# Seven products instead of eight for the second channel product too, in batches 3 to 7 of a fused attention, mixer and gated-MLP kernel

## The chip, the cores and the metric

The kernel runs on one core of one Trainium2 chip. The time is device microseconds of one launch. The engines are named as in the profile: PE (TensorE, matrix products), PEld (its weight loads), DVE (VectorE), ACT (ScalarE), POOL (GpSimd), SP (SyncE, which issues the transfers). PSUM is the memory that PE writes products into; SBUF is the on-chip memory for everything else.

## The reference

Eight batches of 576 tokens and 512 channels go through three blocks in float32, each batch by itself:

```
out  = softmax(q k^T / 8) v          # 8 heads of 64, in chunks of 64 tokens; then x[S=576, 512]
u    = x + (relu(x^T w_tok1) w_tok2)^T           # w_tok1 576x256, w_tok2 256x576
y    = u + relu(u w_ch1) w_ch2                   # w_ch1 512x1536, w_ch2 1536x512
a, v = split(relu(y w_in), 2)                    # w_in 512x1024
g    = a * (w_spatial @ layernorm(v) + b_spatial)
out  = g w_out                                   # 512x512
```

The two products with w_ch1 and w_ch2 are called ch1 and ch2 below. `h` is relu(u w_ch1), 1536 rows by 576 tokens in the transposed form in which the kernel holds it.

## The kernel before

Each float32 operand is held as two f16 numbers, a high part and the rest (hi and lo), and each product of two matrices is made as three PE products: hi·hi, hi·lo, lo·hi. Channels lie on the 128 partitions, tokens along the row, in two halves of 288. One matmul is 128 weights by 128 rows by 288 columns (the first three products) or 512 columns (the others).

One batch passes these stages in the order in which PE is to run them: ch1, ch2, blocks of the output product of the batch before (`proj`, L779, 12 matmuls of 512 columns, called a proj block here), the two halves of the gated MLP's first product (`gate_v` L702 and `gate_u`), then the token mixing of the next batch (tok1 L466, tok2), the spatial product with its multiplication (`gated`, L754 and L766), and then ch1 of the next batch. The attention of a later batch (steps such as L225, L241, L242, L251 to L254, L295 and L296) is cut into about 100 steps, which are placed between the matmuls by a counter of PE columns; the table PACE (L499) says how quickly that counter runs in each stage.

PE's order is the order in which the code issues. The order on DVE, ACT and POOL is made by a scheduler from priorities (`tc.high_priority`) and the times it expects, and each of these engines then works strictly in that order.

From batch 2 on, ch1 (`ch1_fast`, L615) treats the row tiles in six pairs. The weights of a pair form a 2x2 matrix of blocks, and so do the channels and tokens of u; the four block products of h that a 2x2 product needs, eight in the usual way, come from seven products of sums of blocks, called A11, A12, A22, S1, S2, S3, S4 here (the code before has them by numbers 0 to 6). A product of a pair is six matmuls. Four intermediate results are added by DVE: u2 (L645), v (L660), the block c22 (L661) and the two blocks c (L652). ACT applies relu in place (L634), copies the high parts (L503), POOL subtracts for the low parts (L504). The sums of the weights are made once, in batch 1, laid down in DRAM (`c1s`), and streamed by SP through 18 slots of 512 columns (L578). The sums of u are made behind tok2 (`first_sums`, L509 to L523).

The order of one pair p on PE is A11(p), S2(p), S4(p-1), A22(p-1), S1(p), S3(p), A12(p). The two results of a PSUM tile d are S1 and S3 of p; S4(p) is added onto S1's half, so it may begin only when v and c22 have read d. This is the line on which S4 waits:

```
DVE.tensor_tensor(out=vb, in0=d[:, 0, 0:288], in1=u2b[p % 2], op=ALU.add)      # L660
DVE.tensor_tensor(out=c22, in0=d[:, 1, 0:288], in1=vb, op=ALU.add)             # L661
```

ch2 (L669) is the usual product in every batch: 288 matmuls of 288 columns with weights that stay in SBUF (L676), and a residual addition (L535 to L537) for each of the four row tiles.

PSUM tiles come from one ring of four two-bank tiles (`mp`), which attention's scores and outputs use too.

Of the kernel before, what the change touches and what calls it, by code (L numbers as in the profile page):

```python
# [26 lines left out]
def mixer_kernel(ctx: ExitStack, tc, qk0, qk, v, wt1, wt2, wc1, wc2, win, wsp, bsp, wout, out):  # L27
# [471 lines left out]
    PACE = {"first": 0.5, "pair": 0.8, "ch1": 1.0, "ch2": 1.2, "gate": 1.0, "tok1": 1.0, "last": 0.6}  # L499
# [82 lines left out]
    used = [0]

    def sum_steps(p):
        f = vals[:, 0:1024].rearrange("p (k m) -> p k m", k=4)
        s = vals[:, 1024:2048].rearrange("p (n k m) -> p n k m", n=4, k=2)
        g = vall[:, 0:2048].rearrange("p (n e k m) -> p n e k m", n=4, e=2, k=2)
        a11, a12, a21, a22 = f[:, 0:2, 0:128], f[:, 2:4, 0:128], f[:, 0:2, 128:256], f[:, 2:4, 128:256]
        w = c1w[:, :, p]
        o = c1s[p].rearrange("p (n e k m) -> p n e k m", n=7, e=2, k=2)  # L590
# [24 lines left out]
    def ch1_fast():  # L615
        t1, t2 = slice(0, 288), slice(288, 576)
# [3 lines left out]
        def product(o, p, n, b, start):  # L620
            assert ORDER[used[0] % 42] == (p, n)
            i = used[0] % SLOTS * 512
            w = call[:, i:i + 512].rearrange("p (e k m) -> p e k m", e=2, k=2)
            o = o[:, 0:288]
            for k in range(2):
                for i, (a, e) in enumerate(((0, 0), (0, 1), (1, 0))):
                    PE.matmul(out=o, lhsT=w[:, a, k], rhs=b[:, e, k], start=(start and k + i == 0),  # L627
                              stop=(k == 1 and i == 2), skip_group_check=not start)
                    pump(288)
            used[0] += 1  # L630
            stream(used[0] + SLOTS)

        def relu2(c, hi, lo):
            ACT.activation(out=c, in_=c, func=AF.Relu)  # L634
            split(c, hi, lo, POOL)

        for p in range(7):
# [8 lines left out]
            if p:
                d, u = cd[p - 1], u2b[(p - 1) % 2]
                product(d[:, 0], p - 1, 6, xb[:, :, 2:4, t2], False)
                product(d[:, 1], p - 1, 2, tq[3], False)
                c = wrk.tile([128, 2, 288], F32, tag="t", name="c")  # L650
                with high():
                    DVE.tensor_tensor(out=c, in0=d[:, :, 0:288], in1=u.rearrange("p (a t) -> p a t", a=1).to_broadcast([128, 2, 288]), op=ALU.add)  # L652
                    relu2(c, hb[:, p - 1, 0, 1:3], hb[:, p - 1, 1, 1:3])
            if p < 6:
                cd[p] = d = pm.tile([128, 2, 512], F32, tag="m", name="mp")
                c22 = c22b[p % 2]
                product(d[:, 0], p, 3, tq[0], True)
                product(d[:, 1], p, 5, tq[2], True)
                with high():
                    DVE.tensor_tensor(out=vb, in0=d[:, 0, 0:288], in1=u2b[p % 2], op=ALU.add)  # L660
                    DVE.tensor_tensor(out=c22, in0=d[:, 1, 0:288], in1=vb, op=ALU.add)  # L661
                    relu2(c22, hb[:, p, 0, 3], hb[:, p, 1, 3])
                product(a[:, 0], p, 1, xb[:, :, 2:4, t1], False)
                with high():
                    x1, hi, lo = a[:, 0, 0:288], hb[:, p, 0, 0], hb[:, p, 1, 0]
                    ACT.activation(out=hi, in_=x1, func=AF.Relu)
                    DVE.scalar_tensor_tensor(out=lo, in0=x1, scalar=0.0, in1=hi, op0=ALU.max, op1=ALU.subtract)
# [310 lines left out]
```

## Time and profile before

| | |
|---|---|
| three runs | 1149.47, 1152.74, 1153.25 us; median 1152.74 |
| profiled execution | 1149.73 us, span 1147.9 us |
| granted TensorE clock | 0.995 of full speed over the span |
| PE, DVE, ACT, POOL busy | 96%, 57%, 40%, 30% of the span |

The span runs from the first to the last instruction of the profiled execution. PE is busy nearly all the time, so time is lost or won where PE works or where it waits; the other engines matter by what they make PE wait for. Matmuls follow one another faster than a single one lasts, so the cost of a matmul is read from a long run of them, not from the mean duration of one.

### The profile page before, as it was taken

Reading aid. Unit: us, or ns where it says so; the run is one execution under the profiler, and the core shown is the slowest. Engines: PE = TensorE matmul, PEld = TensorE weight load, DVE = VectorE, ACT = ScalarE, POOL = GpSimd, SP = SyncE. Lnnn points to the kernel's source line nnn. Section 1 sums busy time; section 2 is a strip of 40 time slices with the busy share of each in tenths; the row PEclk is TensorE's granted clock in tenths of the full one; section 3 lists DMA queues with packets and bytes.
Section 4 is the critical chain, followed back from the end, with each engine's and each line's share of the span. In section 5 each row is a group of like instructions: output and inputs, shape, how many; then the busy total and the mean of one; then the engine's idle time right before and its main releaser. Section 6 shows DMA issues by size and latency. Waiting matters only on the chain.

```text
span 1147.9 us, 26048 instructions
## 1 busy us (share of the span) xinstructions
PE 1106.4 (96%) x11040; PEld 787.2 (69%) x11040; DVE 651.1 (57%) x1117; ACT 458.6 (40%) x798; POOL 344.6 (30%) x328
## 2 busy tenths in 40 slices
PE   6898999999999999999999999999999999999998
PEld 5576757776577756777567765677657775677765
DVE  7999987666485245744466534763258422562132
ACT  3334444444346233553345423463244612343131
POOL 0000033334254212642235322453135421252021
PEclk9899999999999999999999999999999999999999
DMA  9487521565037250463314532255222612030001
GB/s 320 143 251 238 194 62 29 134 153 157 15 75 188 59 128 3 108 163 72 96 29 129 141 81 70 38 153 129 79 43 71 171 32 61 5 98 14 19 19 46
DMA packets 139108, 115.27 MB, mean 100 GB/s; under 512 B 81520, under 2 KB 122992, under 8 KB 136688
## 3 DMA queue, kind: packets, MB, share of 16 engines
q1 hardware_dynamic: 138992, 113.62, 36.8%
q8 instruction: 86, 1.41, 0.5%
q14 instruction: 30, 0.25, 0.1%
HBM read 84.48 MB, written 14.94 MB: 87 GB/s over the span
## 4 chain that ended last, share of the span: by engine, by line
PE 74%; DVE 18%; issue 3%; ACT 2%; DMA 2%; POOL 1%; SPq 0%; DVEq 0%; ACTq 0%; POOLq 0%
PE mp L676 22%; PE mp L450 16%; PE mp L627 14%; PE mp L779 8%; PE mp L702 7%; PE mp L473 4%; DVE gb L147 2%; DVE gb L143 2%; DVE gt L754 1%; PE mp L234 1%; DVE xT L509 1%; PE mp L280 1%; DVE gb L141 1%; DVE gt L766 1%; DVE qk L225 1%
## 5 line engine op out<-in xcount | busy, mean ns | idle before, releaser
L676 PE MATMUL mp<-hb,c2w 128*128 128x288 f16 x2304 | 289.6, 286 | 4.5 <-DVE c2w L156 4.4
L676 PEld LDWEIGHTS <-c2w 128*128 128x128 f16 x2304 | 222.6, 98 | 62.2 <-DVE c2w L156 5.7
L627 PEld LDWEIGHTS <-c1w 128*128 128x128 f16 x1512 | 147.2, 98 | 50.3 <-issue 13.3
L627 PE MATMUL mp<-xb,c1w 128*128 128x288 f16 x864 | 125.1, 286 | 11.2 <-DVE vn L645 9.0
L450 PE MATMUL mp<-spw,vn 128*128 128x288 f16 x896 | 112.3, 286 | 0.0
L450 PEld LDWEIGHTS <-vn 128*128 128x128 f16 x896 | 87.1, 98 | 22.0
L450 PE MATMUL mp<-xb,inw 128*128 128x288 f16 x768 | 99.4, 286 | 0.6 <-ACT vt L712 0.4
L537 POOL TENSOR_TENSOR xb<-rt,xb 128x576 f16<-128x576 f32 x22 | 29.9, 1359 | 223.6 <-ACT xb L536 223.6
L779 PE MATMUL mp<-otw,gb 128*128 128x512 f16 x432 | 95.4, 379 | 0.0
L450 PEld LDWEIGHTS <-inw 128*128 128x128 f16 x768 | 74.8, 98 | 24.7 <-issue 1.0
L702 PE MATMUL mp<-inw,xb 128*128 128x512 f16 x384 | 88.2, 379 | 0.5 <-ACT xb L536 0.3
L450 PE MATMUL mp<-xb,c1w 128*128 128x288 f16 x576 | 73.8, 286 | 4.4 <-DVE xb L530 2.5
L535 DVE SCALAR_TENSOR_TENSOR rt<-mp,xT 128x576 f32<-128x576 f32 x32 | 24.1, 754 | 93.5 <-PE mp L676 93.5
L779 PEld LDWEIGHTS <-gb 128*128 128x128 f16 x432 | 42.0, 98 | 48.8
L504 POOL TENSOR_TENSOR hb<-c,hb 128x576 f16<-128x576 f32 x36 | 46.1, 1281 | 95.4 <-ACT hb L503 95.4
L718 DVE BATCH_NORM_STATS2 st<-vt 128x6 f32<-128x512 f32 (+1 forms) x40 | 27.5, 690 | 81.2 <-ACT vt L712 76.8
L450 PEld LDWEIGHTS <-c1w 128*128 128x128 f16 x576 | 55.3, 98 | 19.9 <-DVE c1w L156 3.0
L536 ACT ACTIVATE xb<-rt 128x576 f16<-128x576 f32 x32 | 21.9, 684 | 117.0 <-DVE rt L535 117.0
L262 POOL TENSOR_TENSOR p<-sd,p 128x512 f16<-128x512 f32 (+1 forms) x30 | 36.8, 1226 | 97.2 <-ACT p L259 85.8
L702 PEld LDWEIGHTS <-xb 128*128 128x128 f16 x384 | 37.2, 98 | 41.8 <-DVE xb L537 0.7
L627 PE MATMUL mp<-c1w 128*128 128x288 f16 x432 | 64.7, 286 | 0.0
L769 POOL TENSOR_TENSOR gb<-gt,gb 128x576 f16<-128x576 f32 x31 | 48.4, 1566 | 47.0 <-ACT gb L768 47.0
(183 smaller groups left out, 1656.6 us busy)
## 6 DMA issues: line engine op xcount, KB each, us to landing
c1w<-c1s SPq DMA_DIRECT2D x252, 128.0 KB, 2.3
qk<-in_qk SPq DMA_DIRECT2D x96, 128.0 KB, 2.9
out<-o SPq DMA_DIRECT2D x31, 256.0 KB, 2.0
v<-in_v SPq DMA_DIRECT2D x56, 128.0 KB, 2.9
vn<-in_wc SPq DMA_DIRECT2D x4, 1024.0 KB, 5.2
otw<-in_wc SPq DMA_DIRECT2D x3, 1024.0 KB, 4.9
spw<-in_wc SPq DMA_DIRECT2D x3, 1024.0 KB, 5.5
c1s<-vn SPq DMA_DIRECT2D x6, 512.0 KB, 2.9
```

What stands on the lines that cost most here:

```text
L262: POOL.tensor_tensor(out=p_hl[rows, 1], in0=m["sd"][rows], in1=p_hl[rows, 0], op=ALU.subtract)
L450: PE.matmul(out=o, lhsT=l, rhs=r, start=(i == 0), stop=(i == len(seq) - 1))
L473: PE.matmul(out=pss[m], lhsT=l, rhs=r, start=(i + j == 0), stop=False)
L504: eng.tensor_tensor(out=lo, in0=t, in1=hi, op=ALU.subtract)
L535: keep("d", DVE.scalar_tensor_tensor(out=t, in0=ps, scalar=DN10, in1=two(x[:, m]), op0=ALU.mult, op1=ALU.add))
L537: eng.tensor_tensor(out=xl, in0=t, in1=xh, op=ALU.subtract)
L627: PE.matmul(out=o, lhsT=w[:, a, k], rhs=b[:, e, k], start=(start and k + i == 0), stop=(k == 1 and i == 2), skip_group_check=not start)
L676: PE.matmul(out=o, lhsT=c2w[:, a, k, mc], rhs=hb[:, k // 2, r, k % 2 * 2 + t], start=(k + e == 0), stop=(k == 11 and e == 2))
L702: PE.matmul(out=ps, lhsT=l, rhs=r, start=(k + e == 0), stop=(k == 3 and e == len(seq) - 1))
L718: keep("d", DVE.bn_stats(out=st[0:n], in_=t[0:n]))
L769: eng.tensor_tensor(out=gl, in0=t, in1=gh, op=ALU.subtract)
L779: PE.matmul(out=ps, lhsT=gb[:, l, k, tk], rhs=otw[:, r, k], start=(k == 0 and e == 0), stop=(k == 3 and e == 2))
```

## The change

In batches 3 to 7 ch2 is made by seven products per 2x2 block as well. There h takes the part that u has in ch1: besides its four blocks, seven sums and blocks in all are needed in hi and lo for each pair of row tiles, and they are made pair by pair inside `ch1_fast`: xs holds the four blocks in float32, t13 is one DVE subtraction of 576 columns, t24 two of 288, and POOL makes the low parts of the pieces. The results go to the memory that h and the resident ch2 weights had (`hF`). ch2 then is 14 products of 18 matmuls. The sums of w_ch2 are made in batch 2 and laid down in DRAM (`c2s`), and 42 pieces per batch are streamed through the same 18 slots as those of ch1. From batch 2 on, two proj blocks move from behind ch2 to behind the third and the sixth pair of `ch1_fast`; in batches of five blocks the fifth moves to just before `gated`. The order of the gate tiles changes, and PACE has other numbers.

```diff
+    A11, A12, A22, S1, S2, S3, S4 = range(7)
+    ORDER2 = [(0, A11), (1, A11), (0, A12), (1, A12), (0, S2), (0, S1), (0, S3), (1, S2), (1, S1), (1, S3), (0, S4), (0, A22), (1, S4), (1, A22)]
+    FIRST_FAST, FIRST_FULL = 2, 3
+    hF = [t[:, 4032 * i:4032 * (i + 1)].rearrange("p (n e t) -> p n e t", n=7, e=2) for t in (hall, c2all) for i in range(3)]
+    c2s = tc.dram_tile([2, 7, 128, 1536], F16, name="c2s")
...
-    PACE = {"first": 0.5, "pair": 0.8, "ch1": 1.0, "ch2": 1.2, "gate": 1.0, "tok1": 1.0, "last": 0.6}
+    PACE = {"first": 0.2, "pair": 0.8, "ch1": 1.0, "ch2": 1.3, "gate": 1.0, "tok1": 1.0, "last": 0.3}
...
+        pieces += [(1, p, n, 0) for p, n in ORDER1]
+        if b >= FIRST_FULL:
+            pieces += [(2, q, n, k) for q, n in ORDER2 for k in range(3)]
...
+                    c = xp[:, 1:4:2] if full else new_work("c")
+                    DVE.tensor_tensor(out=c, in0=d[:, :, 0:288], in1=spread(u), op=ALU.add)
+                    if full:
+                        f = hF[p - 1]
+                        ACT.activation(out=c, in_=c, func=AF.Relu)
+                        split(xp[:, 2:4], f[:, 1:3, 0], f[:, 1:3, 1], POOL)
+                        t13, t24 = new_work("t13"), new_work("t24")
+                        DVE.tensor_tensor(out=t13, in0=xp[:, 1:3], in1=xp[:, 0:2], op=ALU.subtract)
+                        DVE.tensor_tensor(out=t24[:, 0], in0=xp[:, 2], in1=t13[:, 0], op=ALU.subtract)
+                        DVE.tensor_tensor(out=t24[:, 1], in0=xp[:, 3], in1=t24[:, 0], op=ALU.subtract)
+                        split(t13, f[:, 3:5, 0], f[:, 3:5, 1], POOL)
+                        split(t24, f[:, 5:7, 0], f[:, 5:7, 1], POOL)
...
+                    if full:
+                        xp = xs[p % 2][:, 0]
+                        ACT.activation(out=xp, in_=x1, func=AF.Relu)
+                        split(xp, hF[p][:, 0, 0], hF[p][:, 0, 1], DVE)
...
+            if p in between:
+                between[p]()
+
+    def ch2_fast(x):
+        def product(o, n, start):
+            q, m = next(order)
+            for j in range(3):
+                w = weights_of(2, q, n, j)
+                fast_product(o, w, lambda e, k: hF[2 * j + k][:, blocks[n], e], start and j == 0, j == 2, start)
...
             if b >= FIRST_FAST:
-                ch1_fast()
+                early = pend[:2]
+                pend = pend[2:]
+                ch1_fast(b >= FIRST_FULL, {5 - 3 * k: (lambda i=i: proj(b - 1, i)) for k, i in enumerate(early)})
...
+            if b == FIRST_FULL - 1:
+                sum_pump([(2, p, vall) for p in range(4)], 2000.0)
+            if b >= FIRST_FULL:
+                ch2_fast(x)
...
-            for i in pend:
+            for i in pend[:2]:
                 proj(b - 1, i)
+            if b == FIRST_FULL - 1:
+                sum_end()
+                sum_pump([(2, p, hall) for p in range(4, 6)], 4500.0)
```

On PE the change is plain from this: ch2 of five batches has 252 matmuls instead of 288, and proj blocks stand between pairs. On the other engines the scheduler decides. In batch 7, where no attention is left, DVE's rows from one pair's c to the next stood like this before (L660 and L661 are v and c22, L667 the low part of the block from A12, L645 is u2):

```order
L652 TENSOR_TENSOR c_13386<-mp_13326,vn_97 128x576 [waits PE_49,Pool_49]
L660 TENSOR_TENSOR vn_97<-mp_13391,vn_97 128x288 [waits DVE_49,PE_49]
L661 TENSOR_TENSOR vn_97<-mp_13391,vn_97 128x288 [waits DVE_49]
L667 SCALAR_TENSOR_TENSOR hb_95<-mp_13355,hb_95 128x288 [waits Activation_49]
L645 TENSOR_TENSOR vn_97<-mp_13420,vn_97 128x288 [waits Activation_49]
L652 TENSOR_TENSOR c_13451<-mp_13391,vn_97 128x576 [waits PE_49,Pool_49]
```

and now like this (L713 is c, L719 t13, L732 v, L720 and L721 the two parts of t24, L733 c22, L510 the low part, L706 u2):

```order
L713 TENSOR_TENSOR vn_97<-mp_13766,vn_97 128x2x288 [waits PE_49]
L719 TENSOR_TENSOR t13_13829<-vn_97 128x576 [waits Activation_49,Pool_49]
L732 TENSOR_TENSOR vn_97<-mp_13838,vn_97 128x288 [waits DVE_49,PE_49]
L720 TENSOR_TENSOR t24_13830<-vn_97,t13_13829 128x288 [waits DVE_49,Pool_49]
L733 TENSOR_TENSOR xs_100<-mp_13838,vn_97 128x288 [waits DVE_49]
L721 TENSOR_TENSOR t24_13830<-vn_97,t24_13830 128x288 [waits DVE_49]
L510 TENSOR_TENSOR hb_95<-xs_100,hb_95 128x288 [waits Activation_49]
L706 TENSOR_TENSOR vn_97<-mp_13882,vn_97 128x288 [waits Activation_49]
L713 TENSOR_TENSOR xs_100<-mp_13838,vn_97 128x2x288 [waits PE_49]
```

Three instructions of the pair before, t13 and the parts of t24, have come between c and c22 and between c22 and the next u2, and t13 waits for ACT.

ACT's rows of the same stretch were (L644 copies A11's result for u2, L634 is relu, L503 the high part):

```order
L644 ACTIVATE vn_97<-mp_13420 128x288 [waits PE_49]
L634 ACTIVATE c_13451<-c_13451 128x576 [waits DVE_49]
L503 ACTIVATE hb_95<-c_13451 128x576 [waits Activation_49]
L666 ACTIVATE hb_95<-mp_13420 128x288 [waits PE_49]
L634 ACTIVATE vn_97<-vn_97 128x288 [waits DVE_49]
L503 ACTIVATE hb_95<-vn_97 128x288 [waits Activation_49]
L644 ACTIVATE vn_97<-mp_13485 128x288 [waits PE_49]
```

and are now (L716 relu of c, the three L509 after it high parts, L743 and L735 relus, L948 the copy of a proj block, L705 the copy for u2):

```order
L716 ACTIVATE vn_97<-vn_97 128x2x288 [waits DVE_49]
L509 ACTIVATE hb_95<-vn_97 128x2x288 [waits Activation_49]
L509 ACTIVATE hb_95<-t13_13829 128x2x288 [waits DVE_49]
L743 ACTIVATE xs_100<-mp_13794 128x288 [waits PE_49]
L509 ACTIVATE hb_95<-xs_100 128x288 [waits Activation_49]
L735 ACTIVATE xs_100<-xs_100 128x288 [waits DVE_49,Pool_49]
L509 ACTIVATE hb_95<-t24_13830 128x2x288 [waits DVE_49]
L948 ACTIVATE o_13879<-mp_13866 128x512 [waits DMAHW1_49,PE_49]
L705 ACTIVATE vn_97<-mp_13882 128x288 [waits PE_49]
```

The copy for the next u2 stands behind the copy of t24, which waits for DVE.

At the start of ch1 of batch 3, DVE's last rows ahead of the first u2 were (L252 to L254 are attention, L754 and L766 the spatial product's multiplication):

```order
L252 TENSOR_SCALAR mx_6453<-mx_6453 128x8 [waits DVE_49]
L766 TENSOR_TENSOR gt_6054<-gt_6054,hb_95 128x576 [waits DVE_49]
L253 RECIPROCAL mx_6453<-mx_6453 128x8 [waits DVE_49]
L254 TENSOR_TENSOR sd_6201<-sd_6201,mx_6453 128x512 [waits DVE_49]
L754 SCALAR_TENSOR_TENSOR gt_6095<-mp_6061,bB_83 128x576 [waits PE_49,Pool_49]
L766 TENSOR_TENSOR gt_6095<-gt_6095,hb_95 128x576 [waits DVE_49]
L754 SCALAR_TENSOR_TENSOR gt_6133<-mp_6102,bB_83 128x576 [waits PE_49,Pool_49]
L766 TENSOR_TENSOR gt_6133<-gt_6133,hb_95 128x576 [waits DVE_49]
L645 TENSOR_TENSOR vn_97<-mp_6140,vn_97 128x288 [waits Activation_49]
```

and are now (L258 to L261 attention, L913 and L925 the multiplication):

```order
L258 TENSOR_REDUCE mx_6665<-sd_6418 128x8 [waits Activation_49]
L259 TENSOR_SCALAR mx_6665<-mx_6665 128x8 [waits DVE_49]
L260 RECIPROCAL mx_6665<-mx_6665 128x8 [waits DVE_49]
L261 TENSOR_TENSOR sd_6418<-sd_6418,mx_6665 128x512 [waits DVE_49]
L913 SCALAR_TENSOR_TENSOR gt_6226<-mp_6197,bB_83 128x576 [waits PE_49,Pool_49]
L925 TENSOR_TENSOR gt_6226<-gt_6226,hb_95 128x576 [waits DVE_49]
L706 TENSOR_TENSOR vn_97<-mp_6233,vn_97 128x288 [waits Activation_49]
```

Between the attention's last step and u2 one multiplication stands where there were two.

In the last pair of batch 4, DVE's rows from one c to the next were

```order
L652 TENSOR_TENSOR c_8445<-mp_8376,vn_97 128x576 [waits PE_49]
L660 TENSOR_TENSOR vn_97<-mp_8450,vn_97 128x288 [waits DVE_49,PE_49]
L661 TENSOR_TENSOR vn_97<-mp_8450,vn_97 128x288 [waits DVE_49,Pool_49]
L667 SCALAR_TENSOR_TENSOR hb_95<-mp_8409,hb_95 128x288 [waits Activation_49]
L652 TENSOR_TENSOR c_8495<-mp_8450,vn_97 128x576 [waits PE_49]
```

and from c22 to the next c and t13 are now

```order
L733 TENSOR_TENSOR vn_97<-mp_8613,vn_97 128x288 [waits DVE_49]
L249 TENSOR_TENSOR sd_8782<-mp_8620,mx_8781 128x2x4x64
L232 TENSOR_TENSOR qk16_86<-qk32_85,qk16_86 128x8x64 [waits DMAHW4_49,DMAHW3_49,DMAHW7_49,DMAHW2_49,Activation_49]
L510 TENSOR_TENSOR c2w_79<-vn_97,c2w_79 128x288 [waits Activation_49]
L258 TENSOR_REDUCE mx_8941<-sd_8782 128x8 [waits Activation_49]
L259 TENSOR_SCALAR mx_8941<-mx_8941 128x8 [waits DVE_49]
L260 RECIPROCAL mx_8941<-mx_8941 128x8 [waits DVE_49]
L261 TENSOR_TENSOR sd_8782<-sd_8782,mx_8941 128x512 [waits DVE_49]
L713 TENSOR_TENSOR vn_97<-mp_8613,vn_97 128x2x288 [waits PE_49]
L719 TENSOR_TENSOR t13_8735<-vn_97 128x576 [waits Activation_49,Pool_49]
```

Six attention steps, which before stood one pair earlier, now stand between the last c22 and the last c.

## Rows read from the trace of the kernel before

**Rows 1.** The page, part 1: busy time, share of the span, instructions

```profile
PE 1106.4 (96%) x11040; PEld 787.2 (69%) x11040; DVE 651.1 (57%) x1117; ACT 458.6 (40%) x798; POOL 344.6 (30%) x328
```

**Rows 2.** Waits of PE: line, what it waited for, total, times, longest

```profile
PE mp L627 <- DVE vn L645: 9.0, 5, 2.1
...
PE mp L627 <- DVE vn L661: 2.3, 6, 0.4
```

**Rows 3.** Chain of waits of batch 7: start, length, what

```profile
1047.13 35.28 PE mp L676 x288
1082.41 7.77 PE mp L779 x36
```

**Rows 4.** Timeline, one pair of batch 4 without attention: start, length, engine, line

```profile
623.74 0.46 DVE L661 TENSOR_TENSOR vn<-mp,vn 128x288 f32<-128x288 f32 x1
...
625.19 0.90 PE L627 MATMUL mp<-xb,c1w 128*128 128x288 f16 x6
625.39 0.41 ACT L644 ACTIVATE vn<-mp 128x288 f32<-128x288 f32 x1 [0.23 <-PE mp L627]
...
625.83 0.46 DVE L645 TENSOR_TENSOR vn<-mp,vn 128x288 f32<-128x288 f32 x1 [1.01 <-ACT vn L644]
...
626.86 0.76 DVE L652 TENSOR_TENSOR c<-mp,vn 128x576 f32<-128x576 f32 x1 [0.57 <-PE mp L627]
```

**Rows 5.** Timeline, last pair of batch 4

```profile
640.40 0.46 DVE L661 TENSOR_TENSOR vn<-mp,vn 128x288 f32<-128x288 f32 x1
...
640.92 0.90 PE L627 MATMUL mp<-xb,c1w 128*128 128x288 f16 x6 [0.38 <-DVE vn L661]
```

**Rows 6.** Groups of DVE by shape: busy, mean ns, idle before

```profile
L225 DVE TENSOR_TENSOR qk<-qk,qk 128x1024 f16<-128x1024 f32 x24 | 32.7, 1363 | 0.6 <-ACT qk L222 0.6
L766 DVE TENSOR_TENSOR gt<-gt,hb 128x576 f32<-128x576 f32 x32 | 30.0, 937 | 1.0
L652 DVE TENSOR_TENSOR c<-mp,vn 128x576 f32<-128x576 f32 x36 | 27.2, 755 | 19.5 <-PE mp L627 19.5
...
L754 DVE SCALAR_TENSOR_TENSOR gt<-mp,bB 128x576 f32<-128x576 f32 x32 | 24.0, 751 | 14.8 <-PE mp L450 12.6 <-POOL gb L772 1.5
...
L254 DVE TENSOR_TENSOR sd<-sd,mx 128x512 f32<-128x512 f32 x24 | 16.8, 698 | 0.5
...
L242 DVE TENSOR_TENSOR sd<-mp,mx 128x512 f32<-128x512 f32 x24 | 16.5, 686 | 0.5
...
L251 DVE TENSOR_REDUCE mx<-sd 128x8 f32<-128x512 f32 x24 | 16.3, 678 | 3.5 <-ACT sd L246 3.5
```

**Rows 7.** Groups of POOL by shape

```profile
L504 POOL TENSOR_TENSOR hb<-c,hb 128x576 f16<-128x576 f32 x36 | 46.1, 1281 | 95.4 <-ACT hb L503 95.4
...
L504 POOL TENSOR_TENSOR hb<-vn,hb 128x288 f16<-128x288 f32 x36 | 26.4, 734 | 1.9 <-ACT hb L503 1.9
```

**Rows 8.** Groups of ACT by shape

```profile
L634 ACT ACTIVATE c<-c 128x576 f32<-128x576 f32 x36 | 24.7, 685 | 55.6 <-DVE c L652 55.2
L503 ACT ACTIVATE hb<-c 128x576 f16<-128x576 f32 x36 | 24.6, 683 | 1.0
...
L644 ACT ACTIVATE vn<-mp 128x288 f32<-128x288 f32 x36 | 14.7, 408 | 7.3 <-PE mp L627 7.3
```

**Rows 9.** Timeline of POOL, sums of u before ch1 of batch 2

```profile
321.88 1.60 POOL L299 TENSOR_TENSOR xh<-xT,xh 128x512 f16<-128x512 f32 x1 [1.30 <-issue]
324.89 3.44 POOL L504 TENSOR_TENSOR c1w<-q,c1w 128x576 f16<-128x576 f32 x2 [1.41 <-ACT c1w L503]
```

**Rows 10.** Timeline of DVE, the same stretch

```profile
322.39 1.71 DVE L519 TENSOR_TENSOR q<-xT,q 128x576 f32<-128x576 f32 x1
324.02 0.75 DVE L504 TENSOR_TENSOR xb<-xT,xb 128x576 f16<-128x576 f32 x1
324.69 0.75 DVE L521 TENSOR_TENSOR q<-xT 128x576 f32<-128x576 f32 x1
325.35 1.83 DVE L523 TENSOR_TENSOR q<-xT,q 128x576 f32<-128x576 f32 x1
```

**Rows 11.** The page, part 6: transfers, KB each, median us from issue to landing

```profile
c1w<-c1s SPq DMA_DIRECT2D x252, 128.0 KB, 2.3
```

More of the change, by code (lines that the diff above doesn't have):

```diff
@@ L580, in stream, with weights_of @@
             streamed[0] += 1
[L582 to L590, printed above, removed]
+    def weights_of(*piece):
+        assert pieces[used[0]] == piece
+        used[0] += 1
+        return slot(used[0] - 1).rearrange("p (e k m) -> p e k m", e=2, k=2)
@@ L620, in product, with block, store @@
         def product(o, p, n, b, start):
[L621 to L633, printed above, removed]
+            w = weights_of(1, p, n, 0)
+            fast_product(o, w, lambda e, k: b[:, e, k], start, True, start)
+        def block(p, j):
+            return hb[:, p, 0, j], hb[:, p, 1, j]
+        def store(c, hi, lo, eng=POOL):
             ACT.activation(out=c, in_=c, func=AF.Relu)
-            split(c, hi, lo, POOL)
+            split(c, hi, lo, eng)
         for p in range(7):
@@ L654, in ch1_fast @@
             if p < 6:
[L655 to L658, printed above, removed]
+                cd[p] = d = new_bank()
+                c22 = xs[p % 2][:, 2] if full else c22b[p % 2]
+                product(d[:, 0], p, S1, tq[0], True)
+                product(d[:, 1], p, S3, tq[2], True)
                 with high():
@@ L661, in ch1_fast @@
                     DVE.tensor_tensor(out=c22, in0=d[:, 1, 0:288], in1=vb, op=ALU.add)
[L662 to L667 removed]
+                    if full:
+                        ACT.activation(out=c22, in_=c22, func=AF.Relu)
+                    else:
+                        store(c22, *block(p, 3))
@@ new lines, in ch1_fast @@
+                product(a[:, 0], p, A12, xb[:, :, 2:4, T1], False)
+                with high():
+                    x1 = a[:, 0, 0:288]
+                    if full:
+                        xp = xs[p % 2][:, 0]
+                        ACT.activation(out=xp, in_=x1, func=AF.Relu)
+                        split(xp, hF[p][:, 0, 0], hF[p][:, 0, 1], DVE)
+                    else:
+                        hi, lo = block(p, 0)
+                        ACT.activation(out=hi, in_=x1, func=AF.Relu)
+                        DVE.scalar_tensor_tensor(out=lo, in0=x1, scalar=0.0, in1=hi, op0=ALU.max, op1=ALU.subtract)
@@ L908, in mixer_kernel @@
                 attention_from(b + 2, 0.0, 112000.0)
-                with tc.issue_after(last):
-                    fin()
+                if b == 0:
+                    with tc.issue_after(last):
+                        fin()
                 pace[0] = PACE["last"]
```

195 lines of the change are left out of this document (155 added, 40 removed).

## The prediction, made before the run

> **What bounds the kernel now.** Read the page's engine shares first: PE is busy for 96% of the span, DVE for 57%, POOL for 30% [rows 1]. So matmuls taken out are time taken out, as long as PE finds its next operand ready; the question is what PE will wait for afterwards. Next the list of PE's waits. Two lines of it belong to ch1: 9.0 us in five waits of the first S4 for u2, one at the start of ch1 of each of batches 2 to 6, and 2.3 us in six waits of the last S4 for c22, one at the end of each ch1 [rows 2]. Then the chain of the last batch for the price of a matmul: 288 in 35.28 us, 122.5 ns each, and 36 matmuls of 512 columns in 7.77 us, 216 ns each [rows 3]. Last the timeline of one pair. Undisturbed, a pair is 42 matmuls, 42 x 0.1225 = 5.145 us. There c22 ends at 624.20 and the S4 that needs it starts at 625.19: with 0.06 us of hand-over, as at the end of ch1 where it decides (640.40 + 0.46 to 640.92), the slack is 0.93 us [rows 4, 5]. That slack is all that the new sums may use.
>
> The sum below is made against the profiled execution, 1149.73 us. The median of the three runs, 1152.74, stands 3.0 us higher, so I add 3.0 at the end.
>
> **What goes.** (a) 36 matmuls in each of five batches, 180 x 0.1225 = 22.05 us [rows 3]. All of it lies on the path.
>
> (b) A proj block now stands between the sixth pair's last product and its S4. It is 12 x 0.216 = 2.59 us of work that waits for none of the pair's sums, and more than the 0.38 us of each of the six waits [rows 2, 3]. So 2.3 us go. The bounds are 0 and 2.3.
>
> (c) The start of ch1. In batches 2 to 5 two multiplications, of 0.75 and 0.94 us a piece [rows 6], stand on DVE between the attention's last step and u2; the order now leaves one there in batches 3 and 5, and the first two thirds of the wait go with them. Placing the rows with these durations I get waits of 0.3, 0.55, 2.0, 0.55 and 0 us in batches 2 to 6, so 3.4 is left of 9.0 and 5.5 us are saved. Bounds: 0, if attention only arrives later, and 9.0.
>
> (d) The proj blocks cost the same wherever they stand. Behind ch2 two are left, 5.2 us; they still cover the last residual, which is one addition of 0.75 us, a copy of 0.68 us and one subtraction of 1.28 us, 2.7 us and some hand-overs [rows 6, 7, 8]. I count this as zero. If that cover failed, it would cost under 1 us a batch.
>
> **What comes: the pair's sums.** t13 is one DVE subtraction of 576 columns, t24 two of 288, and POOL gets three subtractions of 1.28 us a pair, 3.84, where it had 1.28 + 0.73 = 2.01 [rows 7]. By their sums alone all engines fit beside 5.145 us of PE. The order is what decides. Set c's start to 0. c takes 0.755 us, relu on ACT 0.685, so t13 begins at 1.50 and ends at 2.25 [rows 6, 8]; v of the next pair ends at about 2.7. ACT's copy of c's high part ends at 2.16, and POOL subtracts from 2.27 to 3.55. The next instruction on DVE is t24's first part, ahead of c22.
>
> Here a row decides what it takes. DVE subtractions with both inputs in SBUF wait while POOL runs: L519 starts at 322.39 under a POOL instruction that runs from 321.88 to 323.48 and takes 1.71 us; L521, the same work begun before POOL starts, takes 0.75; L523 begins at 325.35 under POOL's next and takes 1.83 [rows 9, 10]. 323.48 - 322.39 + 0.75 = 1.84, so the instruction waited for nearly all of POOL's. The group means say the same: the addition that reads PSUM means 751 ns, the multiplication that follows it from SBUF, same shape, 937 [rows 6].
>
> [...]
>
> So t24's first part waits for POOL until about 3.41 and ends at 3.86, c22 ends at 4.24, and S4 can start at 4.30. Undisturbed S4 starts 625.19 + 5.145 - 626.86 = 3.47 after c [rows 4]. PE waits for 0.85 us. The second part then meets POOL's t13 subtraction and ends at 5.31; ACT's copy of t24 (0.68) stands ahead of the copy for the next u2 (0.41) [rows 8], so u2 starts at 6.50 and the next c at 6.87. The loop over pairs takes 6.87 us in place of 5.145. Without the blocking the same placing gives about 5.8.
>
> Two of the five intervals between pairs now hold a proj block, 5.145 + 2.59 = 7.7 us of work on PE, which covers 6.87. The other three wait: 0.9 first, while slack is left, then 1.5 and 1.7, in all 4.1 us a batch, **20.5 us in five batches**. Bounds: 1.0 a batch (the quicker loop, most of it in slack), 5 us; and 5.5 a batch where attention's steps fall in too, 27 us. I take 20.5 since the rows on the blocking are clear and DVE's and ACT's orders are fixed.
>
> **What comes: attention at the end of ch1.** In batch 4 six attention steps on DVE now stand between the last c22 and the last c: 0.686 + 1.363 + 0.678 + 0.2 + 0.2 + 0.698, with the low part's 0.45 between, 4.3 us [rows 6]. Before they stood a pair earlier and beside work that needed less of DVE. Batches 3 and 5 have the like. c holds up the freeing of a PSUM tile and the first operands of ch2. Placing these I get about 2.5 us in batches 3, 4 and 5 for a PSUM tile, 0.4 to 1.7 at ch2's start and about 2.4 in batches 6 and 7, together 11 to 12 us. But the proj block behind the sixth pair covers 2.59 us of each, and some of it is counted in the pair's wait already. I take 6; the bounds are 0 and 12.
>
> **What comes: weights.** The sums of w_ch2 in batch 2 are some 25 instructions on DVE, ACT and POOL for each of six pairs beside an ordinary ch2 on PE, and their transfers. Those of w_ch1 in batch 1 did the same and no line of PE's waits names them, so 0.5 us, with bounds 0 and 4. The stream gets 210 pieces of 128 KB beside 252, at one piece per 0.735 us of PE (6 x 0.1225) as in ch1, each landing in 2.3 us [rows 11], while 18 slots hold 13 us of work: zero. If the cover of 18 slots were gone, each piece would cost up to 2.3 us.
>
> **The sum.** -22.05 - 2.3 - 5.5 + 20.5 + 6 + 0.5 = -2.85: 1149.73 - 2.85 = 1146.9, and in the frame of the median 1149.9. I round to 1149.7, which is **a little faster at best, nearly no change**. What a measurement of this kernel can tell from no change is about 0.3%, 3.5 us.
>
> **Rivals.** (R1) The pair's waits hide. If DVE slips t24 into time in which POOL is idle, because ACT's copies and with them POOL run later than I place them, the quicker loop holds: 5 in place of 20.5 us. Then the sum is -22.05 - 2.3 - 5.5 + 5 + 6 + 0.5 = -18.3, and with the bounds of the end of ch1 -24 to -12, so 1128 to 1140 in the frame of the median, 1134 likeliest. For it: DVE is busy for only 57%, POOL for 30% [rows 1]. Against it: the blocked rows and an order in which t24 comes ahead of c22.
>
> (R2) It gets slower, by one mechanism: DVE's queue at the last two pairs. Attention's 4.3 us stand in front of c there, DVE blocked subtractions behind it, and PE arrives at ch2 before the pieces of the sixth pair are there. If this costs its full 12 us and (c) brings only half, 2.8, the sum is -22.05 - 2.3 - 2.8 + 20.5 + 12 + 0.5 = +5.9, and with the pairs' 27 us it is +12. That is 1156 to 1165, likeliest 1159. It decides from the point at which the end of ch1 costs more than 3 us in each batch. For it: the order, which puts the steps in the last interval, and PSUM's ring of four tiles. Against it: the proj block of 2.59 us at that very place.
>
> (R3) The change doesn't bring the removed matmuls' time because the stream is late, through SP waiting for attention's transposes ahead of it in its queue. A piece that is late once in a batch by 2.3 us costs 11.5 in all, +9. Against it: 13 us of pieces in stock.
>
> **How the numbers follow.** The forecast, -9 to +3 against before (1144 to 1156), has 0.5; R1 0.22; R2 0.25; R3 0.03. Faster by more than 3.5 us: nearly half of the forecast's chance, 0.23, and R1's 0.22: 0.45. Within 3.5: the rest of the forecast's but for a little, 0.24, and a tenth of R2's, 0.03: 0.27. Slower: 0.28. A range that holds 8 in 10 leaves out the lower half of R1 and the upper end of R2 with R3: 1134 to 1161. The forecast's own range is 1144 to 1156.
>
> **What would show it.** In the profile after: ch2 of batches 3 to 7 as a stretch of 252 matmuls in 30.9 us where no wait cuts it (a); no wait of S4 for c22 behind the proj block (b); PE's wait for u2 at the start of ch1 down to about 3.4 us in all (c); a new line of PE's waits, S4 for c22 (L733) or c's chain, of 15 to 25 us in all, in the three intervals without a proj block, with t24's parts (L720, L721) taking 0.8 us or more in the mean where an undisturbed one of 288 columns needs 0.45. If L720 and L721 mean 0.45 and the wait for L733 is under 6 us, R1 is right and my forecast is wrong. If the waits at ch2's start and for PSUM tiles make more than 12 us, R2 is.

## The result: 1.3% slower, and the profile after

The changed kernel took 1167.10 us (median of four runs, 1165.78 to 1168.81), the kernel before beside it 1152.89. The ratio is 1.0131, 95% interval 1.0107 to 1.0154. The prediction was 1149.7 us in a range of 1134 to 1161, so the time is above the range and on the other side of no change.

The page of the changed kernel begins so (busy time, share, instructions):

```profile
span 1164.0 us, 26575 instructions
...
PE 1092.1 (94%) x10860; PEld 769.7 (66%) x10860; DVE 776.7 (67%) x1269; ACT 506.0 (43%) x884; POOL 427.8 (37%) x392
```

Against [rows 1] PE has 14.3 us less to do, with a span 16.1 us longer, and DVE 126 us more. The longest waits of PE (columns as in [rows 2]; L706 is u2, L733 c22, L778 the copy of A11's result at the start of ch2, L303 an attention output whose copy frees a PSUM tile):

```profile
PE mp L667 <- DVE vn L733: 10.7, 13, 1.8
PE mp L667 <- ACT vn L778: 8.9, 5, 3.0
...
PE mp L667 <- DVE xs L733: 5.4, 6, 1.4
PE mp L667 <- DVE vn L706: 5.2, 5, 1.5
PE mp L457 <- ACT hb L487: 3.7, 8, 1.9
PE mp L861 <- ACT xb L542: 3.5, 2, 2.6
PE mp L667 <- ACT xh L303: 3.4, 2, 1.7
```

Where [rows 2] had two lines for ch1, 9.0 and 2.3 us, there are 16.1 us for c22 (two lines, since c22 lies in two buffers), 5.2 for u2 and 8.9 at the start of ch2. A pair like that of [rows 4] looks like this in batch 7 (timeline, no attention):

```profile
1055.11 0.76 DVE L719 TENSOR_TENSOR t<-xs 128x576 f32<-128x576 f32 x1 [0.82 <-ACT xs L716]
...
1055.80 1.28 POOL L510 TENSOR_TENSOR hb<-xs,hb 128x576 f16<-128x576 f32 x1 [2.09 <-ACT hb L509]
...
1056.15 1.25 DVE L720 TENSOR_TENSOR t<-xs,t 128x288 f32<-128x288 f32 x1
...
1057.04 1.49 POOL L510 TENSOR_TENSOR hb<-t,hb 128x576 f16<-128x576 f32 x1
...
1057.32 0.45 DVE L733 TENSOR_TENSOR vn<-mp,vn 128x288 f32<-128x288 f32 x1
1057.68 1.16 DVE L721 TENSOR_TENSOR t<-xs,t 128x288 f32<-128x288 f32 x1
1057.81 0.90 PE L667 MATMUL mp<-xb,c1w 128*128 128x288 f16 x6 [0.90 <-DVE vn L733]
```

L720 starts under a POOL instruction and ends at 1057.40, 0.32 us behind that one's end at 1057.08; c22 (L733) comes after it, and S4 right behind c22, 0.90 us late. L721 goes the same way under POOL's next: it ends at 1058.84, 0.31 us behind it. In batch 5 the same L720 starts 0.29 us ahead of POOL's next instruction (800.09 against 800.38), not under one, and takes 0.44 us. That is the last pair there, on DVE, from behind c22 on:

```profile
800.09 0.44 DVE L720 TENSOR_TENSOR t<-xs,t 128x288 f32<-128x288 f32 x1
800.45 1.76 DVE L232 TENSOR_TENSOR qk<-qk,qk 128x512 f16<-128x512 f32 x1
802.14 1.53 DVE L510 TENSOR_TENSOR c2w<-vn,c2w 128x288 f16<-128x288 f32 x1
803.59 0.45 DVE L721 TENSOR_TENSOR t<-xs,t 128x288 f32<-128x288 f32 x1
803.96 0.67 DVE L258 TENSOR_REDUCE mx<-sd 128x8 f32<-128x512 f32 x1
...
805.11 1.54 DVE L261 TENSOR_TENSOR sd<-sd,mx 128x512 f32<-128x512 f32 x1
806.58 0.74 DVE L713 TENSOR_TENSOR vn<-mp,vn 128x576 f32<-128x576 f32 x1
```

The last c (L713) has eight instructions in front of it since c22 (two short ones are left out here), and three of them, L232, L510 and L261, start under POOL's instructions (800.38 to 801.67, 801.63 to 803.35, 804.83 to 806.10): they take 4.8 us together, where the prediction's durations, 1.363, 0.45 and 0.698, make 2.5. ACT's queue waits for c, and behind that stands the copy for which ch2's third product waits:

```profile
810.23 1.26 PE L667 MATMUL mp<-hb,c1w 128*128 128x288 f16 x9 [2.95 <-ACT vn L778]
```

In batch 7, without attention, ch2 is what [rows 3] promised. The chain there:

```profile
1071.25 32.50 PE mp L667 x264
1103.75 5.18 PE mp L938 x24
```

264 matmuls, 12 of them still ch1's, in 32.50 us are 123 ns each.

### The profile page after: what moved, and what is told of

It reads as the page before. It is cut to its first block, busy times and chain, and to the rows that moved or that the text cites. A ratio compares the mean times of both kernels' runs of the same rounds, so it can differ in the third digit from the quotient of the medians.

```text
span 1164.0 us, 26575 instructions
## 1 busy us (share of the span) xinstructions
PE 1092.1 (94%) x10860; PEld 769.7 (66%) x10860; DVE 776.7 (67%) x1269; ACT 506.0 (43%) x884; POOL 427.8 (37%) x392
## 4 chain that ended last, share of the span: by engine, by line
PE 60%; DVE 23%; ACT 5%; issue 5%; DMA 4%; POOL 2%; SPq 1%; DVEq 0%; ACTq 0%; POOLq 0%
PE mp L457 23%; PE mp L667 17%; PE mp L861 7%; PE mp L938 5%; PE mp L835 3%; PE mp L480 3%; DVE t L720 3%; DVE t L721 2%; DVE gb L154 2%; DVE gb L150 1%; DVE qk L232 1%; PE mp L241 1%; PE mp L287 1%; DMA c2s<-vn 1%; DVE gb L148 1%
## 5 line engine op out<-in xcount | busy, mean ns | idle before, releaser
L667 PEld LDWEIGHTS <-c1w 128*128 128x128 f16 x2772 | 269.8, 98 | 110.8 <-issue 40.4
L667 PE MATMUL mp<-xb,c1w 128*128 128x288 f16 x864 | 125.9, 286 | 24.6 <-DVE vn L733 10.7
L835 PE MATMUL mp<-hb,c2w 128*128 128x288 f16 x864 | 110.3, 286 | 4.2 <-DVE c2w L163 2.7
L835 PEld LDWEIGHTS <-c2w 128*128 128x128 f16 x864 | 82.8, 98 | 26.7 <-DVE c2w L163 4.0
L667 PE MATMUL mp<-hb,c1w 128*128 128x288 f16 x630 | 90.5, 287 | 9.3 <-ACT vn L778 8.9
L861 PE MATMUL mp<-inw,xb 128*128 128x512 f16 x384 | 91.0, 385 | 4.9 <-ACT xb L542 3.5
L667 PE MATMUL mp<-c2w,c1w 128*128 128x288 f16 x630 | 90.4, 288 | 0.0
L457 PEld LDWEIGHTS <-c1w 128*128 128x128 f16 x576 | 56.3, 99 | 20.4 <-issue 2.9
L667 PE MATMUL mp<-c1w 128*128 128x288 f16 x432 | 65.2, 286 | 0.0
L928 POOL TENSOR_TENSOR gb<-gt,gb 128x576 f16<-128x576 f32 x31 | 41.1, 1327 | 60.2 <-ACT gb L927 60.2
L543 POOL TENSOR_TENSOR xb<-rt,xb 128x576 f16<-128x576 f32 x7 | 10.7, 1533 | 140.1 <-ACT xb L542 140.1
L885 POOL TENSOR_TENSOR y<-z,mhalf 128x1 f32<-128x1 f32 (+1 forms) x40 | 24.1, 602 | 92.0 <-DVE z L884 70.0
```

Of the source, the lines that this page charges most:

```text
L457: PE.matmul(out=o, lhsT=l, rhs=r, start=(i == 0), stop=(i == len(seq) - 1))
L667: PE.matmul(out=o[:, 0:288], lhsT=w[:, a, k], rhs=b(e, k), start=(start and k + i == 0), stop=(stop and k == 1 and i == 2), skip_group_che ...
L835: PE.matmul(out=o, lhsT=c2w[:, a, k, mc], rhs=hb[:, k // 2, r, k % 2 * 2 + t], start=(k + e == 0), stop=(k == 11 and e == 2))
L861: PE.matmul(out=ps, lhsT=l, rhs=r, start=(k + e == 0), stop=(k == 3 and e == len(seq) - 1))
L885: POOL.tensor_tensor(out=y[0:n], in0=z[0:n], in1=mhalf[0:n], op=ALU.pow)
L928: eng.tensor_tensor(out=gl, in0=t, in1=gh, op=ALU.subtract)
```

## The experiments

Theory 1 is that three separate things cost the time: the sums of w_ch2 in the first three batches, t24 held up by POOL in each pair, and attention in front of the last c. "Against before" is the ratio to runs of the kernel before on the same chip; waits and spans are of the profiled execution. Line numbers shift a little between the kernels; the names in brackets say which is meant.

### The rest of the change alone

```diff
-    FIRST_FAST, FIRST_FULL = 2, 3
+    FIRST_FAST, FIRST_FULL = 2, 8
-                sum_pump([(2, p, vall) for p in range(4)], 2000.0)
-                sum_pump([(2, p, hall) for p in range(4, 6)], 4500.0)
```

> The change without its core: ch2 stays the usual product in every batch and no sums of w_ch2 are made; the moved proj blocks, the order of the gate tiles and PACE are as in the changed kernel. Theory 1 (what was lost comes from the sums and their use, not from the rest): the last S4 no longer waits (-2.3 us), the waits for u2 at the start of ch1 shrink from 9 to about 4, so 4 to 8 us faster than before. Rival (two proj blocks behind ch2 no longer cover the last residual, and PACE moves attention to a worse place): 3 to 10 us slower than before.

1143.32 us, 0.9921 (0.9900 to 0.9942), span 1139.5. The waits for c22 are down to 0.5 us. Those for u2 are down to 3.6: 0.5 under their own name and two of 1.5 under that of a load of attention, though PE starts right behind u2 there (the last two rows, timeline of batch 3):

```profile
PE mp L667 <- DMA qk<-in_qk: 3.1, 2, 1.5
...
PE mp L667 <- DVE vn L733: 0.5, 2, 0.3
...
PE mp L667 <- DVE vn L706: 0.5, 1, 0.5
```

```profile
474.40 0.45 DVE L706 TENSOR_TENSOR vn<-mp,vn 128x288 f32<-128x288 f32 x1
...
474.90 1.63 PE L667 MATMUL mp<-xb,c1w 128*128 128x288 f16 x12 [1.52 <-DMA qk<-in_qk]
```

Theory 1 holds: the moved proj blocks and the placing of attention are a gain of 8.4 us in span, by themselves.

### The sums made and not used

```diff
-    FIRST_FAST, FIRST_FULL = 2, 3
+    FIRST_FAST, FIRST_FULL = 2, 8
-            if b == FIRST_FULL - 1:          # at the three places that make the sums
+            if b == 2:
```

> As the run before it, but the sums of w_ch2 are made and stored as in the changed kernel, and not used. Theory 1 (the sums cost what the first three batches of the changed kernel lost, a wait of 2.6 us in batch 0 for a weight load behind the early copies, some 4.5 us of waits in batch 2, and a lowered clock after both): 8 to 11 us more than the run without sums. Rival (those waits have other causes, the sums cost what was predicted, 0.5 us with at most 4): 0 to 4 us more.

1150.69 us, 0.9989 (0.9977 to 1.0002), 7.4 us more than without sums, the span 9.1 us more (1148.6). The waits that return are those of the gate stage and of tok2:

```profile
PE mp L457 <- ACT hb L487: 3.7, 8, 1.9
PE mp L861 <- ACT xb L542: 2.5, 2, 1.9
PE mp L861 <- DVE xb L543: 1.6, 2, 1.4
```

By the medians that is just under the expected 8 to 11, by the spans inside it, and far from the rival's 0 to 4. Of the 9.1 us, 2.1 were lost before the gate stage of batch 0 begins (144.01, without sums 141.87). The run below with the copies in batch 1 begins it at 144.61 with no copy before it, so this part is not shown to be the sums' doing.

### POOL relieved

```diff
-                        split(xp[:, 2:4], f[:, 1:3, 0], f[:, 1:3, 1], POOL)
+                        ACT.activation(out=f[:, 1:3, 0], in_=xp[:, 2:4], func=AF.Copy)
-                        split(t13, f[:, 3:5, 0], f[:, 3:5, 1], POOL)
+                        ACT.activation(out=f[:, 3:5, 0], in_=t13, func=AF.Copy)
```

> The changed kernel, but in batches 3 to 7 POOL makes no low part of c and t13 (ch2 reads the high part in their place, so it runs as many matmuls); DVE's order stays. Theory 1 (t24 is blocked by POOL, and by this alone the pair takes 6.72 us): L720 and L721 fall from 1.0 to 1.3 us to 0.45 in the mean, the waits of S4 for c22 from 16.1 us to under 6, and the time by 9 to 14 us against the changed kernel. Rival (the place of t24 ahead of c22 and the hand-overs between DVE and ACT are enough): waits of over 11 us stay, and the time falls by under 5.

This run leaves the low parts of c and t13 out of the result; it measures POOL's part alone, and DVE's order in batches 3 to 7 is the changed kernel's, instruction by instruction. 1137.03 us, 0.9874 (0.9851 to 0.9897): the span fell by 28.4 us (1135.6), twice the upper end of what was expected. DVE's groups (the second column is the mean in ns) and PE's waits:

```profile
L720 DVE TENSOR_TENSOR t<-vn,t 128x288 f32<-128x288 f32 x15 | 7.4, 492 | 0.2
L721 DVE TENSOR_TENSOR t<-vn,t 128x288 f32<-128x288 f32 x15 | 6.8, 453 | 0.2
```

```profile
PE mp L667 <- ACT vn L778: 3.7, 3, 2.0
...
PE mp L667 <- DVE vn L733: 0.6, 2, 0.3
```

In the changed kernel the same two groups read

```profile
L720 DVE TENSOR_TENSOR t<-vn,t 128x288 f32<-128x288 f32 x15 | 19.1, 1276 | 0.5
L721 DVE TENSOR_TENSOR t<-vn,t 128x288 f32<-128x288 f32 x15 | 19.0, 1265 | 0.2
```

So POOL's two subtractions account for nearly all of the 16.1 us, and for 5.2 of the 8.9 at ch2's start, which I had put down to attention alone.

### Attention kept out of the last two pairs

```diff
-            pace[0] = PACE["first" if p < 1 else "pair"]
+            pace[0] = PACE["first" if p < 1 else "pair"] if p < 4 or not full else 0.0
-            pace[0] = PACE["ch2"]
+            pace[0] = PACE["ch2"] if b < FIRST_FULL else 1.57
```

> The changed kernel, but in batches 3 to 7 no attention step is placed in the last two pairs of ch1; ch2 gets them (PACE of ch2 1.57 there). Theory 1 (attention's steps in front of the last c make the waits for ACT's copy at the start of ch2, 8.9 us, and for a PSUM tile, 4.6): both together fall under 4 us, and the time by 7 to 11 us against the changed kernel. Rival (the same steps make PE wait wherever they are put, or the start of ch2 waits for the pair's own sums): the time changes by under 3 us.

1159.04 us, 1.0062 (1.0038 to 1.0086), 8.1 us less than the changed kernel. L778's waits fell from 8.9 to 1.2 us, L303's lines are gone; those for c22 stayed (17.5). As expected. With the run before: attention and POOL both stretch DVE's queue in front of the last c, and taking either away helps.

### The sums moved

The copies of w_ch2's blocks were put on SP behind the pieces streamed beside batch 2's ch1, and all six pairs beside ch2 of batch 2.

```diff
-                sum_pump([(2, p, vall) for p in range(4)], 2000.0)
+                sum_pump([(2, p, vall) for p in range(6)], 2600.0)
-                        SP.dma_start(out=c2s[:, n, ...], in_=w[:, e, k:k + 2, c:c + 128])
+                        with tc.issue_after(tail_sp[0]):
+                            SP.dma_start(out=c2s[:, n, ...], in_=w[:, e, k:k + 2, c:c + 128])
```

> The changed kernel with the sums of w_ch2 elsewhere: SP issues the copies of its blocks into DRAM behind the first streamed pieces of batch 2 in place of batch 0, and all six pairs are summed beside ch2 of batch 2, none behind it. Theory 1 (the copies held up a weight load in batch 0, and the two pairs behind ch2 held up the last residual and tok1 in batch 2): the waits named ACT L542, DVE L543 and ACT L487 go back to the size of before, and the time falls by 6 to 9 us against the changed kernel. Rival (the sums' work costs PE the same wherever it stands): it falls by under 3 us.

1176.90 us, 1.0213 (1.0194 to 1.0233): slower by 9.8 us, a miss. ch1 of batch 2 begins at 334.33, as before the change (334.38; 337.55 in the changed kernel), so batch 0 was cured. But the chain of sums ran over into tok1: with one room each pair waits for the store of the one before (the last row shows it for the second pair), and the copies stand on SP between these stores.

```profile
PE mp L457 <- ACT hb L487: 6.7, 8, 4.9
...
391.48 1.22 DVE L616 TENSOR_TENSOR vn<-c2w 128x1024 f32<-128x1024 f16 x1 [6.37 <-DMA c2s<-vn]
```

### The same instructions in another order

```diff
+                        if rest:
+                            rest.pop()(cop)            # t24's second part of the pair before, behind c
                         t13, t24 = new_work("t13"), new_work("t24")
...
                         ACT.activation(out=c22, in_=c22, func=AF.Relu)
+                        if p:
+                            first(cop)                 # t24's first part, behind c22
+                            rest.append(last)
```

> The changed kernel with the same instructions, but DVE's and the other engines' order forced in batches 3 to 7: t24's first part behind c22 in place of ahead of it, its second part and its copies behind the next pair's c, in the time in which DVE waited for ACT's relu. Theory 1 (POOL blocks t24, and S4 waits only because t24 stands ahead of c22 and of the next u2): the waits of S4 for c22 fall from 16.1 us to under 4, those at ch2's start somewhat too, and the time falls by 12 to 20 us against the changed kernel. Rival (DVE and POOL together have too much work for one pair, 5.9 us against 5.1, wherever it stands): the waits only move to other instructions and the time falls by under 6 us.

Here `first` and `last` make the two parts of t24, each issued behind the instruction that it is given. 1144.69 us, 0.9941 (0.9921 to 0.9961), 22.4 us less than the changed kernel and faster than before. The wait for c22:

```profile
PE mp L667 <- DVE vn L744: 2.4, 2, 2.0
```

The rival, too much work for DVE and POOL in one pair, falls: it was the order.

### The three cures together

The edits of the last three runs, and the low part of A12's block made from PSUM.

> The three cures together, the sums moved, the order forced, attention kept out of the last two pairs, and the low part of the block from A12 made from PSUM as before. Theory 1 (the three losses are separate and add): 25 to 32 us faster than the changed kernel, so 1135 to 1142 and faster than both. Rival (what one cure frees another wait takes): not below 1146.

1144.50 us, 0.9936 (0.9919 to 0.9953): faster than both kernels, but outside the expected 1135 to 1142 and the rival's 1146 or more. The moved sums, a loss in themselves by their own run, are in it (L487 5.7 us here), and the order alone was as fast.

### The copies in batch 1

```diff
+                        with tc.issue_after(stores[2]):
+                            SP.dma_start(out=c2s[:, n, ...], in_=w[:, e, k:k + 2, c:c + 128])
```

> The changed kernel, but the copies of w_ch2's blocks into DRAM stand on SP behind the third store of batch 1's sums, in place of between the weight loads of batch 0; the sums stay where they are. Theory 1 (these copies hold up the load of the spatial weights in batch 0, and PE's wait there lowers the clock): the wait for ACT L542 in batch 0, 2.6 us, goes down to 0.3 and the start of batch 2's ch1 moves ahead by 3 us; 3 to 4 us faster than the changed kernel. Rival (the wait has another cause): no change.

1170.87 us, 1.0170 (1.0144 to 1.0195), 3.8 us slower than the changed kernel, a miss. In the traces the time from batch 0's gate stage to batch 1's is 2.6 us shorter (134.91 against 137.55), but from batch 1's to batch 2's it is 4.0 longer (142.25 against 138.26); 2.2 us more were lost before, where this run has no copy. The gate stage of batch 0 is whole, but that of batch 1 now waits. On SP a transpose of attention stands behind nine copies (4.73 us of issuing), and ACT waits for it:

```profile
273.20 4.73 SPq L625 DMA_DIRECT2D c2s<-c2w  x9
...
278.55 1.33 SPq L270 DMA_TRANSPOSE pT<-p  x1
...
281.78 0.63 ACT L266 ACTIVATE p<-sd 128x512 f16<-128x512 f32 x1 [4.75 <-DMA pT<-p]
```

The copies cost where something urgent stands behind them on SP, here 4.75 us of ACT's time.

### Order, sums in two lots, attention out

The forced order, low part from PSUM, three pairs of sums beside ch2 in each of batches 2 and 3, seven products in ch2 from batch 4 on:

```diff
-    FIRST_FAST, FIRST_FULL = 2, 3
+    FIRST_FAST, FIRST_FULL = 2, 4
-                sum_pump([(2, p, vall) for p in range(4)], 2000.0)
+                sum_pump([(2, 3 * (b - FIRST_FAST) + p, vall) for p in range(3)], 2000.0)
```

> The forced order, the low part of the block from A12 from PSUM, the copies behind the third store of batch 1, and the sums of w_ch2 in two lots of three pairs beside ch2 of batches 2 and 3, so that only batches 4 to 7 use the seven products in ch2. Theory 1 (beside ch2 three pairs fit, what runs over into the gate stage costs): against the forced order alone 3 us less for the copies, 5 to 6 less for batch 2, 2 to 4 more for batch 3, so 1136 to 1141. Rival (the sums cost PE the same in any place): 1144 or more.

1137.36 us, 0.9875 (0.9848 to 0.9903).

> As the run before it, and no attention step in the last two pairs of ch1 in batches 4 to 7. Theory 1 (the steps there hold up c and the PSUM tile also when t24 is no longer blocked): 3 to 6 us faster than the run before. Rival (with the forced order the copies at ch2's start come in time, and the steps cost as much inside ch2): within 2 us of it.

1133.53 us, 0.9841 (0.9816 to 0.9867), 3.8 less again. Both as expected, and both beat both kernels.

> As the run with two lots of sums and no attention in the last two pairs, but each pair's copies of w_ch2's blocks stand on SP behind the store of that pair's sums, in batches 2 and 3, in place of batch 1. Theory 1 (the copies hold up whatever stands behind them on SP, weight loads in batch 0, attention's transposes in batch 1; beside ch2 nothing urgent stands there): batch 2's ch1 begins 6 to 8 us earlier, near 334.5 as in the kernel before, and the time falls by 5 to 8 us, to about 1127. Rival (here they hold up the stores of the sums or the stream, as when all stood behind the stream): within 2 us, or slower.

1134.86 us, 0.9850 (0.9829 to 0.9871): no change against the last, the rival's number but not its reason. ch1 of batch 2 begins at 336.74 in place of 342.00, but that is no gain of the copies: this execution was already 6.1 us ahead at the gate stage of batch 0 (141.96 against 148.03), before any copy in either run. From there to the gate stage of batch 1 it lost 3.2 us: the load of the spatial weights came 1.5 us later than without sums, though no copy stood near it, and PE waited 2.07 us. From that to batch 2's it gained 2.4, where the copies had stood. And in batch 3 the copies do on SP what they did in batch 1, with a transpose of attention behind six of them:

```profile
549.90 3.98 SPq L648 DMA_DIRECT2D c2s<-c2w  x6
...
553.99 1.24 SPq L270 DMA_TRANSPOSE pT<-p  x1
...
556.82 0.63 ACT L266 ACTIVATE p<-sd 128x512 f16<-128x512 f32 x1 [3.31 <-DMA pT<-p]
...
558.08 0.60 PE L880 MATMUL mp<-inw,xb 128*128 128x512 f16 x2 [1.31 <-ACT xb L542]
```

From the gate stage of batch 3 to ch1 of batch 4 it takes 2.9 us more than the last run (56.36 against 53.48).

### t24 by instructions with one input

```diff
-                        DVE.tensor_tensor(out=t24[:, 0], in0=xp[:, 2], in1=t13[:, 0], op=ALU.subtract)
+                        DVE.tensor_scalar(out=t24[:, 0], in0=t13[:, 0], scalar1=2.0, scalar2=None, op0=ALU.mult)
```

and the second part alike. So it leaves out the sums themselves and measures the blocking alone.

> The changed kernel with the same order, but the two parts of t24 are instructions with one input in SBUF (a multiplication by 2 of t13 and of the first part) in place of subtractions with two. Theory 1 (only DVE instructions with two inputs in SBUF are blocked by POOL): L720 and L721 fall from 1.0 to 1.3 us to 0.45 or less in the mean, though POOL does all its work, the waits of S4 for c22 fall from 16.1 us to under 4, and the time by 15 us or more against the changed kernel. Rival (POOL slows any DVE instruction that reads SBUF): the means stay over 0.8 us, and the time falls by under 5.

1158.22 us, 1.0050 (1.0031 to 1.0070), 8.9 us less than the changed kernel, between the two expectations. The waits for c22 are 11.4 us, not under 4. The theory's form was too narrow:

```profile
L720 DVE TENSOR_SCALAR t<-t 128x288 f32<-128x288 f32 x30 | 32.0, 1068 | 0.5
```

Three of sixty, L720 and L721 together, take only 0.29 us; the means are 1.07 and 1.06, and an L720 begun at 1053.52 under a POOL instruction (1053.17 to 1054.45) ends at 1054.61. So it is blocked as well, and saves only what it takes less itself. The rival, any instruction that reads SBUF, falls too: L733, with one input in SBUF and one in PSUM, keeps its 0.45.

## Why the prediction was wrong

Spans of the runs split the loss by the prediction's own terms:

| step | predicted | measured in span |
|---|---|---|
| proj block behind the sixth pair and start of ch1 (b, c) | -7.8 | -8.4 (rest alone against before) |
| sums of w_ch2 and their transfers | +0.5, at most 4 | +9.1 (sums unused against rest alone) |
| matmuls removed, pairs, end of ch1 | -22.05 + 20.5 + 6 = +4.5 | +15.4 (changed kernel against sums unused) |
| together | -2.85 | +16.1 |

**The step that failed first** is "Those of w_ch1 in batch 1 did the same and no line of PE's waits names them, so 0.5 us". In batch 1 the six pairs stand beside ch1 and ch2; in batch 2 they have only ch2, and two pairs were left over for the gate stage and tok1, where the first instruction of one (L616, 1.21 us) stood on DVE in front of the last residual's low part. The copies, 36 transfers early on SP, had no price of their own in the prediction (and a pair's sums are 7 instructions on DVE, ACT and POOL, not some 25). In the changed kernel itself ch1 of batch 3 begins 9.1 us later than with the rest alone (479.40 against 470.28). That the copies hold up the load in batch 0 rests on many runs: with them there PE waits 1.9 to 2.9 us in six of six, without them at most 0.7 in seven of eight, and 2.1 in the last of the runs with two lots.

Behind these waits stands a second price: behind PE's 2.58 us without work in batch 0 the granted clock is 0.66 in the next 5 us (1.00 in the same window with the rest alone), and 0.65 in 4 us after the two waits in batch 2 (0.90 and 1.44). Not every wait has it: behind the 1.98 us at ch2's start in batch 4 the clock is 0.57 in 4 us, but behind the 2.95 us in batch 5 it stays at 1.00 (windows; the column before the last two is the clock):

```profile
150.00:155.00 5.00, 4.96 (x15) 1.74 (x16) 4.88 (x7) 2.34 (x5) 0.00 (x0) 0.66 0.52 119
424.00:428.00 4.00, 4.00 (x17) 1.94 (x16) 2.89 (x8) 1.03 (x2) 3.38 (x4) 0.65 0.72 212
...
669.00:673.00 4.00, 4.00 (x21) 2.56 (x20) 1.59 (x2) 1.37 (x3) 2.10 (x2) 0.57 0.74 216
...
810.00:815.00 5.00, 4.24 (x34) 3.25 (x34) 2.49 (x3) 1.60 (x4) 3.71 (x4) 1.00 0.54 163
```

**The second** is the end of ch1, "I take 6; the bounds are 0 and 12". The waits there are 8.9 (L778), 4.6 (L303, in two lines, 3.4 and 1.2) and 0.3 us: 13.8, above the upper bound. That the placed sum, "11 to 12 us", is near is luck: ch2's start cost 8.9 us in five waits where "0.4 to 1.7" was placed, the PSUM tile 4.6 in three where 2.5 a batch was, and batches 6 and 7 cost 0.3 where "about 2.4" was. What was wrong is the length of DVE's queue in front of c, priced too low (in batch 5 three instructions, started under POOL's, took 4.8 us instead of 2.5), and the cover by the proj block: in batch 5 that block stands ahead of S4, and PE still waits 2.95 us at ch2's third product.

**The pair's sums** were right in mechanism and nearly in size: 16.1 us by PE's waits, of 20.5; in batch 7 0.65, 0.90 and 1.42 us in the three intervals without a proj block, 0.29 in one with. A wait's line counts from the end of the last matmul, 0.286 us after its start (the mean of one below), while in a run the next starts after 0.123; so each wait costs about 0.16 us more than its line, an estimate from these two, and the 19 waits for c22 19.2 us.

```profile
L667 PE MATMUL mp<-xb,c1w 128*128 128x288 f16 x864 | 125.9, 286 | 24.6 <-DVE vn L733 10.7
```

The blocking by POOL was shown by relieving POOL (L720 from 1276 to 492 ns in the mean) and by the order (the waits for c22 from 16.1 to 2.4 us).

**Right**: 123 ns a matmul in the new ch2, the two places where waits went (b, c) as long as ch2 stays as it was, the stream. The start of ch1 (c) was 3.6 us with the rest alone, where 3.4 was forecast, but 5.2 in the changed kernel. Of the third line's 15.4 us the lines of PE's waits explain -22.05 + 15.6 + 13.8 + 1.6 = 8.95; 28 more waits at 0.16 us are 4.6, and the clock of 0.57 in batch 4 is 1.7 (4 us at 0.43 less): 15.2 in all, so nearly all of it.

R2 named the side and the place, and its sign came: the waits at ch2's start and for PSUM tiles are 13.5 us, more than 12. Its price, +6 to +12, lacked the sums and the clock. R1's condition never arose (L720 and L721 mean 1.02 to 1.28 us, not 0.45), since DVE and POOL were pressed together by their order, however idle in the mean.

## What to carry to other kernels

DVE and POOL, busy for 67% and 37% of the span, still set the pace here where their order put a piece that can wait in front of one that PE waits for; with the same instructions, the order alone was worth 22 us. A preparation that cost nothing in one stage has to be priced in the stage to which it is moved, with its transfers' place in the queue. A wait of PE can cost more than its line, and the trace has to say whether it does: behind 2.58 us the clock cost some 1.7 us more here (an estimate, 5 us at 0.66), behind 2.95 us nothing.

## What the runs showed of the hardware

A DVE multiplication by a constant with one f32 input of 128x288 in SBUF is blocked by POOL as well, where I had expected only instructions with two: in the run with one input it took 0.29 us at its shortest and 1.07 in the mean. In the same run c22 (L733), with one input in PSUM, kept its 0.45 us. And the same load of the spatial weights in batch 0 came 1.5 us apart in two kernels without a copy ahead of it: ACT takes it at 143.07 with the rest alone, and at 144.54 in the run with the copies behind the sums.
